# First batch's loads and exponentials placed in the arrays of the later channel weights, with a written list for its steps

## The chip, the cores and the metric

The kernel runs on one NeuronCore of a Trainium2 chip. The metric is the device time of one execution in microseconds, median of three runs. The engines are named as the profile names them: PE is TensorE (matrix products), PEld its weight loads, DVE VectorE, ACT ScalarE, POOL GpSimd, SP SyncE, which only issues DMAs here.

## What is computed

Windowed attention with block summaries, then a mixer over tokens and channels, on four batches of 768 tokens, 8 heads of 64. Cut to what matters:

```
k_sum = max of k over blocks of 32 tokens ; v_sum = mean of v over the same blocks      (24 of each)
a     = softmax over [ q k^T / 8 within |i - j| < 16 ,  q k_sum^T / 8 + log 32 ]
x     = a [v ; v_sum]                     per head; the heads side by side: 768 x 512 per batch
u     = x + (relu(x^T w_tok1) w_tok2)^T   w_tok1 768 x 256, w_tok2 256 x 768
out   = u + relu(u w_ch1) w_ch2           w_ch1 512 x 1536, w_ch2 1536 x 512
```

The weights arrive as 64-bit floats (two 32-bit words each) and are turned into 32-bit ones in the kernel, the channel and second token weights as a high and a low part, so that three fast products stand for one exact one.

## The kernel before

**A plan sets every order.** The code adds pieces of work (`Plan.add`): an engine, an estimated time, what it reads and writes, a rank. `Plan._order` walks them as a small model of the engines would, and the order that comes out is fixed for each engine, SP's queue included. So the places of the instructions follow from the estimates, the ranks and the order in which the pieces are added. A wait at the head of an engine's list holds up all that stands behind it.

**Attention of one pair of heads** (`p`; batch 0 has pairs 0 to 3): `load_k`, `load_q`, `load_v` (L270) bring k (120 columns for each of 12 tiles of 64 queries: a window of 96 keys and 24 places for block maxima), q and two v. `key_blocks` on DVE takes the block maxima (`ks`, L313) and copies them into k (L322). `scores` does one half `g` of the tokens: 12 products into two banks (`sc`, L428), then six times DVE's masked row minimum (L442, called "lowest" here) and ACT's exponential (L452). `turn` transposes the exponentials on PE (`et`, L490), and ACT copies them out (`eT`, L501). `first_means` (batch 0 alone) forms the block means of v on PE (`vm`, 24 products, L340); ACT copies the 24 sums out (`vs`, L360), POOL spreads them into v (L347). `weighted` multiplies with v (`av`, L559) and DVE scales by the reciprocal of the row sums (`x`, L570). An f32 product in the listing is two matrix instructions in the trace: 24 listed are x48 there.

**Token mixer**: `tok1` (`t1p`, L692, ACT L673, DVE L678) and `tok2` (`up`: transposes L849 and products L857; ACT `u` L894, DVE `u` L899).

**Channel mixer**: for each of 12 blocks `f` of the hidden width `ch1` (`hp`, L917, 12 products; ACT and DVE split `h`, L929 and L934) and `ch2` (`acc`, L960, 12 products).

**Weights** come in 30 ticks (`w_tick`): two DMAs (L1092), ACT takes the magnitude (L1122), POOL clamps (L1126), DVE does shift, sign and low word (L1131, L1138, L1145), ACT writes the high part (L1169) and POOL the low one (L1175). Ticks 0 to 5 are token weights, 6 + 2f and 7 + 2f the channel weights of block f. Each tick's words wait in borrowed buffers: tags `u0`, `k`, `q`, `v`, `x`, two buffers each but for `u0` (four).

**The start.** The first steps are added in a loop over a fixed order of scores, turns and products, with the ticks put in at five places; 21 products of a zero tile (`warm`, L1188) run ahead of the first scores. k, q and v have two buffers each, so that the loads for pairs 2 and 3 wait until earlier pairs have been used. The channel weights have four arrays of their own for the whole kernel, `w1h`, `w1l`, `w2h`, `w2l`, which are empty until the ticks fill them. Attention of a later batch is added between the channel steps of the batch ahead of it.

Of the kernel before, what the change touches and what calls it, by code (L numbers as in the profile page):

```python
# [20 lines left out]
DM = H * D  # L21
# [38 lines left out]

class Work:
# [6 lines left out]
class Plan:  # L68
    LATE = {"pe": 0.3, "act": 0.15, "dve": 0.15, "pool": 0.2, "sp": 0.0}
    RATE, LAND = 250.0, 2.2  # L70
# [11 lines left out]
    def add(self, eng, took, run, reads=(), writes=(), rank=0, behind=(), kb=0):  # L82
# [12 lines left out]
        for key in (*reads, *writes):  # L95
            s = key[0]
# [92 lines left out]
def tile_attention_mixer(  # L189
# [77 lines left out]

    def load(slot, view, src, kb, reads=(), behind=()):
# [5 lines left out]
    def load_q(p):  # L274
        b, hp = divmod(p, NP)
        q_t[p] = sbuf([P, S], "q", f"q_{p}", 2)
        return load(q_t[p], lambda t: t, q[b, hp], 393)

    def load_k(p):
        b, hp = divmod(p, NP)  # L280
        k_t[p] = sbuf([P, NT, NC], "k", f"k_{p}", 2)
        return load(k_t[p], lambda t: t, kw[b, hp], 737)

    def load_v(n):
# [5 lines left out]
        tag = "h" if b == 0 and hp % 2 == 1 else "v"  # L290
        slot = v_t[n] = sbuf([P, NT, D], tag, f"v_{n}", 2)
# [37 lines left out]
    def first_means(p):  # L329
# [5 lines left out]
        at = (WIN - 32, WIN)  # L335

        def sums():
            for t in range(NT):
                for j in range(2):
                    nc.tensor.matmul(  # L340
                        pt.t[at[j] : at[j] + NB, :D],
                        lhsT=means[:, NB - 2 - 2 * t : 2 * NB - 2 - 2 * t],
                        rhs=v_t[2 * p + j].t[:WIN, t], start=(t == 0), stop=(t == NT - 1),
                    )

        def spread(n, j):
            nc.gpsimd.tensor_copy(  # L347
                v_t[n].t[WIN:NC],
# [4 lines left out]
            "pe", 1.6, sums, reads=[(v_t[2 * p], 0), (v_t[2 * p + 1], 0)], writes=[(pt, 0)],  # L353
            rank=R_H,
        )
        for j in range(2):
            n = 2 * p + j
            add(
                "act", 0.25,
                lambda j=j: nc.scalar.activation(  # L360
                    s.t[WIN:NC, j * D : (j + 1) * D], pt.t[at[j] : at[j] + NB, :D], AF.Copy
                ),
                reads=[(pt, 0)], writes=[(s, j)], rank=R_EVAC,
            )
# [986 lines left out]
```

## Time and profile before

| what | before |
|---|---|
| median of three runs | 574.99 us (574.8, 574.99, 577.88) |
| profiled execution: span from first to last instruction | 572.0 us |
| around the span (median less span) | 3.0 us |
| PE busy in the span | 561.5 us, 98% |
| DVE, ACT, POOL busy | 278.3, 215.4, 157.9 us |
| mean granted TensorE clock | 0.997 |
| DMA | 75.89 MB, mean 133 GB/s |
| first channel product starts | at 65.31 us |

The profiled execution is one run; its span is what the views below divide up, and the 3.0 us around it are what the runs' times hold besides. Times in views are counted from the span's start. In the chain and the timeline a row reads: start, duration, engine, tile, line, number of instructions. In the tables by stretch, "busy (x)" stands for each engine's busy time and its instructions, then the granted clock, the busy share of the DMA engines and what they moved.

### The profile page before, as it was taken

The page shows a single profiled execution, that of the slowest core. Times are in us where ns is not written, and L with a number is a line of the kernel's source. Part 1 is how long each engine was busy: PE and PEld are TensorE (multiplying, and loading weights), DVE is VectorE, ACT ScalarE, POOL GpSimd, SP SyncE. Part 2 cuts the span into 40 slices and gives each one's busy share as a digit, 9 for nine tenths or more (in the row PEclk, how much of TensorE's full clock was granted, in tenths as well). Part 3 has the DMA queues.
Part 4 walks back from the last instruction along what each step waited for, and adds up shares of the span by engine and source line. Part 5 has one row for each costly group of instructions (what it writes and reads, how often), then busy time and mean ns, then how long its engine had stood idle before and what let it go on. Part 6 is the DMA issues. An engine that isn't in the chain of part 4 may idle for free.

```text
span 572.0 us, 12221 instructions
## 1 busy us (share of the span) xinstructions
PE 561.5 (98%) x4629; PEld 495.9 (87%) x4629; DVE 278.3 (49%) x845; ACT 215.4 (38%) x711; POOL 157.9 (28%) x232
## 2 busy tenths in 40 slices
PE   7899999999999999999999999999999999999997
PEld 3688888889999978877899887878899999999997
DVE  3588899978563364454621455442640422112112
ACT  3776776526474342332314343322423312111110
POOL 0437687824034410000236011100066022005000
PEclk9899999999999999999999999999999999999999
DMA  8953677745465146757856138745542022001001
GB/s 275 325 175 115 204 226 249 251 119 185 152 182 166 37 150 152 208 129 194 220 153 135 16 68 219 198 131 114 136 136 63 14 52 43 1 0 57 0 1 55
DMA packets 116778, 75.89 MB, mean 133 GB/s; under 512 B 86640, under 2 KB 100080, under 8 KB 116720
## 3 DMA queue, kind: packets, MB, share of 16 engines
q1 hardware_dynamic: 116432, 74.72, 46.4%
q8 instruction: 36, 0.59, 0.4%
q10 hardware_dynamic: 288, 0.39, 0.2%
q14 instruction: 22, 0.18, 0.1%
HBM read 57.59 MB, written 15.73 MB: 128 GB/s over the span
## 4 chain that ended last, share of the span: by engine, by line
PE 87%; DVE 3%; ACT 2%; SPq 2%; DMA 2%; POOL 1%; issue 1%; DVEq 0%; ACTq 0%; POOLq 0%
PE hp L917 33%; PE acc L960 33%; PE up L857 5%; PE sc L428 4%; PE av L559 4%; PE t1q L776 3%; SPq L532 2%; PE t1q L739 2%; PE warm L1188 1%; PE et L490 1%; ACT e L452 1%; PE up L849 1%; DMA xT<-xaway 1%; POOL ot L1021 1%; DVE e L442 1%
## 5 line engine op out<-in xcount | busy, mean ns | idle before, releaser
L960 PE MATMUL acc<-h,w2h 128*128 128x512 f32 (+2 forms) x768 | 206.0, 338 | 0.1
L917 PE MATMUL hp<-u,w1h 128*128 128x512 f32 (+2 forms) x768 | 192.8, 338 | 0.0
L960 PEld LDWEIGHTS acc<-h,w2h 128*128 128x128 f32 x768 | 135.5, 188 | 14.0 <-ACT h L929 1.6
L917 PEld LDWEIGHTS hp<-u,w1h 128*128 128x128 f32 x768 | 132.6, 189 | 12.5 <-issue 1.3
L934 DVE SCALAR_TENSOR_TENSOR h<-hp,h 128x512 fp32r<-128x512 f32 (+2 forms) x96 | 53.2, 554 | 156.9 <-ACT h L929 156.7
L917 PE MATMUL hp<-u,w1l 128*128 128x512 f32 (+2 forms) x384 | 129.0, 336 | 0.0
L960 PE MATMUL acc<-h,w2l 128*128 128x512 f32 (+2 forms) x384 | 128.4, 334 | 0.0
L929 ACT ACTIVATE h<-hp 128x512 fp32r<-128x512 f32 (+2 forms) x96 | 47.0, 489 | 199.7 <-PE hp L917 198.7
L452 ACT ACTIVATE e<-e,den 128x120 f32<-128x120 f32 x192 | 73.3, 384 | 55.1 <-DVE den L442 51.8
L917 PEld LDWEIGHTS hp<-u,w1l 128*128 128x128 f32 x384 | 72.4, 189 | 5.8
L960 PEld LDWEIGHTS acc<-h,w2l 128*128 128x128 f32 x384 | 72.2, 188 | 5.3
L442 DVE CUSTOM_DVE_ANT_0 e<-sc,mask_sb 128x120 f32<-128x120 f32 x192 | 41.6, 277 | 20.9 <-PE sc L428 19.7
L1021 POOL TENSOR_TENSOR ot<-ot,u 128x512 f32<-128x512 f32 (+2 forms) x28 | 27.9, 1018 | 84.9 <-DVE ot L1013 83.3
L857 PE MATMUL up<-wt2h,t 128*128 128x256 f32 (+2 forms) x128 | 37.3, 350 | 0.2 <-DVE xT L873 0.2
L452 ACT ACTIVATION_READ_ACCUMULATOR e<-e,den 128x1 f32 x192 | 36.2, 188 | 0.0
L565 POOL TENSOR_SCALAR rec<-den 128x6 f32<-128x6 f32 x32 | 8.6, 269 | 90.8 <-ACT e L452 88.6
L428 PE MATMUL sc<-k,q 64*64 64x120 f32 x768 | 28.1, 273 | 2.2 <-ACT eT L501 0.9
L428 PEld LDWEIGHTS sc<-k,q 64*64 64x64 f32 x768 | 20.5, 133 | 10.5 <-issue 6.1
L559 PEld LDWEIGHTS av<-v,eT 120*64 120x64 f32 x768 | 24.0, 138 | 4.9 <-issue 2.5
L559 PE MATMUL av<-v,eT 120*64 120x64 f32 x768 | 26.6, 224 | 1.0 <-ACT eT L501 0.9
L411 POOL MEMSET e<- 128x48 f32 x16 | 2.2, 139 | 91.4 <-PE av L559 42.0
L857 PEld LDWEIGHTS up<-wt2h,t 128*128 128x128 f32 x128 | 23.1, 188 | 2.6 <-DVE xT L873 0.5
(81 smaller groups left out, 603.4 us busy)
## 6 DMA issues: line engine op xcount, KB each, us to landing
w<-in_w_ch SPq DMA_DIRECT2D x48, 256.0 KB
k<-in_kw SPq DMA_DIRECT2D x16, 720.0 KB
v<-in_vw SPq DMA_DIRECT2D x32, 288.0 KB
q<-in_q SPq DMA_DIRECT2D x16, 384.0 KB
away<-e SPq DMA_DIRECT2D x16, 384.0 KB
eT<-away SPq DMA_DIRECT2D x64, 96.0 KB
w<-in_w_tok SPq DMA_DIRECT2D x12, 256.0 KB
vb<-in_vb SPq DMA_DIRECT2D x32, 96.0 KB
```

The costliest lines, as they stand in the source:

```text
L428: nc.tensor.matmul(tiles[j].t[c * QT : (c + 1) * QT, i * NC : (i + 1) * NC], lhsT=qt.t[rows, t * QT : (t + 1) * QT], rhs=kt.t[rows, t, :], ...
L442: nc.vector.tensor_tensor_reduce(out=e.t[:, j, i * P : i * P + NC], in0=tiles[j].t[:, i * NC : (i + 1) * NC], in1=mask_sb[:, mv, :], op0=A ...
L452: nc.scalar.activation(ei, ei, AF.Exp, bias=den_t[n].t[:, 1, T : T + 1], scale=-1.0, accum_out=den_t[n].t[:, 0, T : T + 1],)
L532: nc.sync.dma_start(out=view()[rows].rearrange("p (t q c) -> p t q c", q=P // 32, c=32), in_=src[..., rows],)
L559: nc.tensor.matmul(pv[cs, T], lhsT=eT[:NC, T % (TT // 2), cs], rhs=v.t[:NC, 2 * T + c], start=True, stop=True,)
L776: nc.tensor.matmul(pt.t.rearrange("p (a c) -> p a c", c=P), lhsT=ws.t[:, wp, T % 2, k * P : (k + 1) * P], rhs=xs.t[:, xp], start=(T == 0 a ...
L857: nc.tensor.matmul(pt.t[:, :nt], lhsT=t1.t[:, part, ks], rhs=w[:, k, h0 : h0 + nt], start=(far and k == 0 and i == 0), stop=(k == DTOK // ...
L917: nc.tensor.matmul(pt.t[:, :nt], lhsT=w[:, c, fs], rhs=us[c].t[:, part], start=(i == 0), stop=(i == len(ops) - 1),)
L929: lambda: nc.scalar.activation(h.t[:, 0], pt.t[:, :nt], AF.Relu),
L934: lambda: nc.vector.scalar_tensor_tensor(out=h.t[:, 1], in0=pt.t[:, :nt], scalar=0.0, in1=h.t[:, 0].bitcast(F32), op0=ALU.max, op1=ALU.sub ...
L960: nc.tensor.matmul(slot.t[:, c0 : c0 + nt], lhsT=w[:, f, o * P : (o + 1) * P], rhs=h.t[:, part], start=(f == 0 and w is w2h and part == 0 ...
L1021: lambda view=view, u=u: nc.gpsimd.tensor_tensor(out=view(), in0=view(), in1=u.t[:, 1].bitcast(F32), op=ALU.add),
```

## The change

Four things are done at once; nothing of what is computed changes.

1. The four channel-weight arrays become 16 tiles of three blocks each. For groups 1 to 3 of each, the same memory first holds a tile of batch 0 (`early`): all four q in group 1 of `w1h` and `w1l`, the four k in group 2 of all four, the eight v in group 3, and in group 1 of `w2h` and `w2l` four of the exponentials (five of the eight steps use these). The weights of a group wait, as the plan sees it, until batch 0's users of that memory are done. With a home of their own, k, q and v of batch 0 need no buffer to come free. The transposed exponentials of batch 0 take the buffers of tags `q` and `v`.
2. The loop of the start becomes a written list of words: `l` loads of a pair, `k` block maxima, `m` block means, `s` scores, `e` turn, `a` weighted, `t` and `u` the token mixer, `w` a tick. Nine ticks stand in it, ten in the loop before. The plan's estimates of the DMA rate (250 to 320), of some steps and of the warm-up change with it.
3. The block means go to four column groups of PE where they went to two: even and odd tiles add up apart. ACT copies the even half out as before, and DVE adds the odd half to it (eight new small additions).
4. 14 warm-up products, 21 before.

```
+    early = {
+        (n, g): plan.slot(sb, [P, WG * DM], F32, f"{n}_{g}", f"early_{n}_{g}", 1)
+        for n in NW for g in range(1, NF // WG)
+    }
...
     def load_k(p):
         b, hp = divmod(p, NP)
-        k_t[p] = sbuf([P, NT, NC], "k", f"k_{p}", 2)
+        if b == 0:
+            k_t[p] = early_part(NW[p], 2, 0, (NT, NC))
+        else:
+            k_t[p] = sbuf([P, NT, NC], "k", f"k_{p}", 2)
...
                 for j in range(2):
+                    c = 2 * j + t % 2
                     nc.tensor.matmul(
-                        pt.t[at[j] : at[j] + NB, :D],
+                        pt.t[32 * c : 32 * c + NB, :D],
                         lhsT=means[:, NB - 2 - 2 * t : 2 * NB - 2 - 2 * t],
-                        rhs=v_t[2 * p + j].t[:WIN, t], start=(t == 0), stop=(t == NT - 1),
+                        rhs=v_t[2 * p + j].t[:WIN, t], start=(t < 2), stop=(t >= NT - 2),
                     )
...
+        def whole(j):
+            nc.vector.tensor_tensor(
+                out=s.t[WIN:NC, j * D : (j + 1) * D], in0=half(j, 1),
+                in1=s.t[WIN:NC, j * D : (j + 1) * D], op=ALU.add,
+            )
...
-        for _ in range(21):
+        for _ in range(14):
             nc.tensor.matmul(pw.t, lhsT=warm.t[:, :P], rhs=warm.t, start=True, stop=True)
...
+    START = (
+        "l0 l1 l2 w k0 k1 s00 s01 s10 e00 k2 s11 w m0 m1 e01 l3 s20 w a0 e10 e11 s21 w e21 "
+        "a1 m2 k3 t1 m3 w w e20 s30 s31 a2 w w t2 e31 e30 t0 u0 u2 a3 u1 t3 w u3"
     )
```

What the plan makes of it is shown at three places. First the head of SP's queue, where all loads are issued; k, q and v carry the pair's or head's number in the old names, and in the new ones the array and group whose memory they take (`early_w1h_2` is k of pair 0, `early_w1l_2` k of pair 1, `early_w2h_2` k of pair 2, `early_w1h_1` q of pairs 0 and 1, `early_w1h_3` v of heads 0 and 1). Before:

```order
L270 DMA k_0_85<-in_kw 128x1440
L270 DMA q_0_87<-in_q 128x768
L1194 DMA mask_sb_71<-in_mask 128x360
L270 DMA k_1_90<-in_kw 128x1440
L270 DMA q_1_92<-in_q 128x768
L270 DMA v_0_94<-in_vw 96x768
L270 DMA v_1_96<-in_vw 96x768
L270 DMA v_2_98<-in_vw 96x768
L270 DMA v_3_122<-in_vw 96x768
L270 DMA k_2_165<-in_kw 128x1440
L270 DMA q_2_167<-in_q 128x768
L1092 DMA w_0_170<-in_w_tok1 128x512 x2
```

The same place now:

```order
L300 DMA early_w1h_2_81<-in_kw 128x1440
L300 DMA early_w1h_1_83<-in_q 128x768
L1253 DMA mask_sb_71<-in_mask 128x360
L300 DMA early_w1h_3_86<-in_vw 96x768 x2
L300 DMA early_w1l_2_89<-in_kw 128x1440
L300 DMA early_w1h_1_83<-in_q 128x768
L300 DMA early_w1l_3_92<-in_vw 96x768 x2
L300 DMA early_w2h_2_110<-in_kw 128x1440
L300 DMA early_w1l_1_112<-in_q 128x768
L300 DMA early_w2h_3_114<-in_vw 96x768 x2
L1147 DMA w_0_117<-in_w_tok1 128x512 x2
L1147 DMA w_1_120<-in_w_tok1 128x512 x2
```

The first nine loads are the same nine; v of heads 0 and 1 has moved ahead of k and q of pair 1, and v of heads 4 and 5 ahead of the token weights.

Second, PE's list around the block means `vm` of pairs 0 and 1 (heads 0 to 3; the exponentials of pair 0 are `e_0` in the old names, `early_w2h_1` in the new). Before:

```order
L340 MATMUL vm_0_230<-v_0_94,means_72 24x64
L340 MATMUL vm_0_230<-v_1_96,means_72 24x64
L490 MATMUL et_0_1_269<-identf_66,e_0_1_177 120x128 x3
L490 MATMUL et_1_1_275<-identf_66,e_0_1_177 120x128 x3
L340 MATMUL vm_1_283<-v_2_98,means_72 24x64
...
L559 MATMUL av_0_313<-v_0_94,eT_0_0_202 64x64 x6
L559 MATMUL av_0_313<-v_0_94,eT_0_1_281 64x64 x6
L559 MATMUL av_1_330<-v_1_96,eT_1_0_205 64x64 x6
L559 MATMUL av_1_330<-v_1_96,eT_1_1_308 64x64 x6
L428 MATMUL sc_2_1_347<-k_1_90,q_1_92 64x120
```

The same place now:

```order
L377 MATMUL vm_1_263<-early_w1l_3_92,means_72 24x64 x24
L540 MATMUL et_0_1_297<-identf_66,early_w2h_1_172 120x128 x3
L482 MATMUL sc_2_1_305<-early_w1l_2_89,early_w1h_1_83 64x120
...
L540 MATMUL et_1_1_327<-identf_66,early_w2h_1_172 120x128 x3
L609 MATMUL av_0_334<-early_w1h_3_86,eT_0_0_238 64x64 x6
L609 MATMUL av_0_334<-early_w1h_3_86,eT_0_1_323 64x64 x6
L609 MATMUL av_1_353<-early_w1h_3_86,eT_0_0_238 64x64 x6
L609 MATMUL av_1_353<-early_w1h_3_86,eT_0_1_323 64x64 x6
L377 MATMUL vm_2_376<-early_w2h_3_114,means_72 24x64 x24
```

The means of pair 1 stand ahead of the second turn of pair 0, and the second half of pair 1's scores, which followed the products with v, stands ahead of them.

Third, SP's queue at the ticks of the third channel block (`w_10`, tick 10) and of the fifth (`w_14`). Before:

```order
L1092 DMA w_12_890<-in_w_ch1 128x2x256 x2
L1092 DMA w_13_933<-in_w_ch2 128x512 x2
L1092 DMA w_10_985<-in_w_ch1 128x2x256 x2
L1092 DMA w_14_0_989<-in_w_ch1 128x2x256
L1092 DMA w_14_1_991<-in_w_ch1 128x2x256
```

The same place now:

```order
L1147 DMA w_12_871<-in_w_ch1 128x2x256 x2
L1147 DMA w_13_898<-in_w_ch2 128x512 x2
L1147 DMA w_14_0_957<-in_w_ch1 128x2x256
L1147 DMA w_14_1_959<-in_w_ch1 128x2x256
L1147 DMA w_10_974<-in_w_ch1 128x2x256 x2
```

Tick 14's two loads, which wait for the words of tick 8 to be used, now stand ahead of tick 10's. On PE, everything from the first `up` on to the end of batch 0's first half stands in nearly the order of before (two `up` have changed places); after that, steps of later batches move by one or two places.

More of the change, by code (lines that the diff above doesn't have):

```diff
@@ L266, in tile_attention_mixer, with early_part, weight, block @@
     q_t, k_t, v_t, vs, vb_t = {}, {}, {}, {}, {}
+    NW, WG = ("w1h", "w1l", "w2h", "w2l"), 3
+    early = {
+        (n, g): plan.slot(sb, [P, WG * DM], F32, f"{n}_{g}", f"early_{n}_{g}", 1)
+        for n in NW for g in range(1, NF // WG)
+    }
+    wt = {
+        (n, g): plan.slot(sb, [P, WG, DM], F32R, f"{n}_{g}", f"{n}_{g}", 1)
+        for n in NW for g in range(NF // WG)
+    }
+    def early_part(n, g, i, shape):
+        size = shape[0] * shape[1]
+        return Part(
+            early[n, g],
+            lambda t: t[:, i * size : (i + 1) * size].rearrange("p (a b) -> p a b", b=shape[1]),
+        )
+    def weight(n, f):
+        return wt[n, f // WG].t[:, f % WG]
+    def block(n, f, c):
+        return weight(n, f)[:, c * P : (c + 1) * P]
     def load(slot, view, src, kb, reads=(), behind=()):
@@ L475, in turn @@
         e = e_t[p, g]
-        if p >= NP:
-            pair = sbuf([P, 2, HS], "e", f"eT_{p}_{g}", 3)
+        tag, bufs = ("e", 3) if p >= NP else (("q", 2), ("v", 2))[g]
+        pair = sbuf([P, 2, HS], tag, f"eT_{p}_{g}", bufs)
         for j in range(2):
@@ L613, in att_step @@
                 turn_x(b, hp)
-            ahead = 1 if b > 0 else 2
-            if b > 0 or hp + ahead < NP:
+            ahead = 1
+            if b > 0:
                 load_v(2 * (p + ahead))
@@ L905, in tile_attention_mixer, with weight_keys @@
     h_t = {}
+    def weight_keys(names, f):
+        return [(wt[n, f // WG], (f, i)) for n in names for i in range(2)]
     def ch1(b, half, f):
@@ L914, in products @@
         def products():
-            ops = [(c, w, part) for c in range(NC4) for w, part in ((w1h, 0), (w1h, 1), (w1l, 0))]
+            ops = [(c, w, part) for c in range(NC4) for w, part in (("w1h", 0), ("w1h", 1), ("w1l", 0))]
             for i, (c, w, part) in enumerate(ops):
                 nc.tensor.matmul(
-                    pt.t[:, :nt], lhsT=w[:, c, fs], rhs=us[c].t[:, part],
+                    pt.t[:, :nt], lhsT=block(w, f, c), rhs=us[c].t[:, part],
                     start=(i == 0), stop=(i == len(ops) - 1),
@@ L923, in ch1 @@
             "pe", 12 * nt / 2220, products,
-            reads=[(u, i) for u in us for i in range(2)] + [("w1", f, 0), ("w1", f, 1)],
+            reads=[(u, i) for u in us for i in range(2)] + weight_keys(("w1h", "w1l"), f),
             writes=[(pt, 0)], rank=R_W,
@@ L1046, in tile_attention_mixer, with halves @@
     w_ch1v = w_ch1.rearrange("(c p) f -> p c f", p=P)
+    def halves(names, f, i):
+        return [lambda n=n: weight(n, f)[:, 256 * i : 256 * (i + 1)] for n in names] + [
+            (wt[n, f // WG], (f, i)) for n in names
+        ]
     for T in range(TT):
-        jobs.append((w_tok1v[:, T : T + 1, :], wt1[:, T - T % 2 : T - T % 2 + 2, :], None, ("wt1", T // 2)))
+        jobs.append((w_tok1v[:, T : T + 1, :], None, None, None, ("wt1", T // 2)))
     for i in range(3):
@@ L1096, in w_tick @@
             )
-        first, rank = two[0][2] is None, R_ATT if i < TOKT else R_W
+        first, rank = two[0][1] is None, R_ATT if i < TOKT else R_W
         psum = i >= 10
```

183 lines of the change are left out of this document (97 added, 86 removed).

## The prediction

> **What bounds the kernel now.** I read the page first, then PE's waits by stretch, then the chain of waits through the first 75 us, then DVE's waits there.
>
> ```profile
> PE 561.5 (98%) x4629; PEld 495.9 (87%) x4629; DVE 278.3 (49%) x845; ACT 215.4 (38%) x711; POOL 157.9 (28%) x232
> PE   7899999999999999999999999999999999999997
> ```
>
> PE is busy nearly throughout; the two slices of 14.3 us that are not full are the first two. PE's longest wait of the start (to 65.3 us), and the only one of all the rest: what waited and for what, total, times, longest:
>
> ```profile
> PE et L490 <- ACT e L452: 2.0, 4, 0.7
> ```
> ```profile
> PE up L857 <- DVE xT L873: 0.2, 1, 0.2
> ```
>
> After 65.3 us PE waits 0.2 us in all: there the time is PE's work, 572.0 - 65.3 = 506.7 us, and the change leaves that work alone. What can be won lies ahead of the first channel product. The chain of waits through the start:
>
> ```profile
> 1.17 7.54 PE warm L1188 x21
> 8.71 0.85 PE sc L428 x24
> 13.16 1.42 PE sc L428 x24
> 14.59 2.69 PE vm L340 x48
> 17.28 0.80 PE et L490 x6
> 18.08 1.46 PE vm L340 x48
> 19.54 1.55 PE av L559 x48
> 21.09 0.78 PE sc L428 x24
> 51.19 0.59 PE up L849 x4
> 56.88 2.68 PE t1p L692 x24
> 65.31 5.46 PE hp L917 x24
> ```
>
> Three marks: scores from 8.7, the first `up` at 51.2, the first channel product `hp` at 65.3. From `up` on the chain is PE alone (14.1 us, the same instructions before and after), so the question is when `up` begins. Between scores and `up` the engines were busy (us, in the first columns):
>
> ```profile
> 9.54:51.80 42.26, 37.09 (x677) 31.55 (x670) 31.83 (x139) 33.53 (x136) 18.99 (x28) 0.96 0.74 229
> ```
>
> 42.3 us, of which PE worked 37.1, DVE 31.8, ACT 33.5. No engine is full; each waits for the others in turn. I take DVE's list as the measure, because it ends with `x` of the last head (51.8), which stands beside the first `up`, and because it is the list to which the change adds work. Its waits in this stretch are 42.26 - 31.83 = 10.4 us:
>
> ```profile
> DVE e L442 <- PE sc L428: 5.8, 3, 3.3
> DVE x L570 <- PE av L559: 4.9, 2, 4.3
> DVE t L678 <- ACT t L673: 1.4, 2, 1.2
> ```
>
> (3.3 of the first row lie ahead of 9.54.) Two of them come early, the second behind slow PE work:
>
> ```profile
> 14.61 0.28 DVE L442 CUSTOM_DVE_ANT_0 e<-sc,mask_sb 128x120 f32<-128x120 f32 x1 [1.35 <-PE sc L428]
> 20.43 0.56 DVE L570 TENSOR_TENSOR x<-av,rec 128x384 f32<-128x384 f32 x1 [4.35 <-PE av L559]
> ```
>
> So 5.7 us are waited up to 20.4 and 4.7 after it.
>
> **The change, part by part.**
>
> *Warm-up.* The 21 products by stretch:
>
> ```profile
> 1.17:7.03 5.86, 5.86 (x14) 2.09 (x15) 1.00 0.89 311
> 7.03:8.64 1.61, 1.61 (x8) 0.59 (x6) 1.00 0.97 380
> ```
>
> The first 14 take 5.86 us (0.42 each), the last seven 1.6 (0.22). Scores wait for nothing else here: k of pair 0 is ready with DVE's copy at 6.25.
>
> ```profile
> 5.94 0.31 DVE L322 COPY k<-ks 128x288 f32<-128x288 f32 x1
> ```
>
> Seven fewer: scores at 7.05 instead of 8.64, **-1.6 us**, all on the path. Bounds: no gain if the mask or q came late (q was issued second, and both queues' places are unchanged), and never more than 1.6.
>
> *Block means.* The row 18.08 has 48 matrix instructions in 1.46 us at full clock, 30 ns each, in two column groups; with four side by side the least is half, 0.73, the most 1.46. The scores use four quarters of the array already: 24 of 120 columns in 0.78 (row 21.09), 33 ns each, which for 64 columns makes 17 ns and 0.84 for 48. I take 0.8. PE saves 0.7 per pair, 2.6 in four, but only pair 1's means stand ahead of a turn that others wait for. The Trainium skill, "TensorE: Matmul & The Clock Gate", section "Wait — 56ns, not 53.3ns?", says that starts of matrix instructions never come closer than about 25 ns, however small they are. By that rule the 48 would take 1.2 us, and as an estimate the total would come out 0.4 us later. The trace shows no four column groups, so the sum keeps 0.8.
>
> *The added half.* ACT's eight small copies stay; DVE gets eight additions of 24x64. None is in the trace; nearest are ACT's copy of the same 24x64 (216 ns) and DVE's reciprocals (178 ns).
>
> ```profile
> L360 ACT ACTIVATE vs<-vm 24x64 f32<-24x64 f32 x8 | 1.7, 216 | 2.9 <-PE vm L340 2.8
> L585 DVE RECIPROCAL rec<-rec 128x6 f32<-128x6 f32 x8 | 1.3, 178 | 0.4 <-POOL rec L565 0.2
> ```
>
> I take 0.2: **+1.6 us** of DVE's list (bounds 1.0 and 2.5).
>
> *Loads at once.* What landed when is bounded by what the DMA engines moved:
>
> ```profile
> 0.00:14.50 14.50, 11.60 (x99) 5.64 (x99) 5.61 (x31) 5.92 (x24) 0.75 (x7) 0.97 0.90 277
> k<-in_kw SPq DMA_DIRECT2D x16, 720.0 KB
> v<-in_vw SPq DMA_DIRECT2D x32, 288.0 KB
> q<-in_q SPq DMA_DIRECT2D x16, 384.0 KB
> mask_sb<-in_mask SPq DMA_DIRECT2D x1, 180.0 KB
> 4.95 0.95 DVE L313 TENSOR_REDUCE ks<-k 128x24 f32<-128x768 f32 x1 [3.19 <-DMA k<-in_kw]
> ```
>
> The engines are 90% busy and move 277 GB/s. The first nine loads (2 k, 2 q, 4 v, mask) are 3540 KB, 3.63 MB, 13.1 us at that rate; the first k (0.74 MB, issued at 0.72) would take 2.7 and was there at 4.95, 1.5 later. So I add 1.5: k of pair 1 is sixth instead of fourth and lands at about 11, its q at 12.4, the last v of pair 1 at 14.6. Loading all at once therefore doesn't speed up the first 15 us; it takes away the later waits of loads for buffers.
>
> Three stretches of 3.4 us, with the granted clock third from the end:
>
> ```profile
> 10.36:13.77 3.41, 1.93 (x21) 1.28 (x25) 2.87 (x20) 3.41 (x17) 0.00 (x0) 1.00 1.07 261
> 13.77:17.19 3.42, 3.42 (x66) 2.94 (x58) 1.47 (x14) 3.00 (x16) 0.47 (x2) 0.50 0.99 357
> 17.19:20.60 3.41, 3.41 (x94) 3.12 (x94) 0.17 (x1) 2.48 (x10) 2.33 (x3) 1.00 0.98 358
> ```
>
> From 13.8 to 17.2 PE has half clock (the mean of 2.69 us against 1.46 and the scores of 1.42 against 0.78 in the chain are from there).
>
> *The new list, early part.* With those landings: DVE starts its minima at 8.0, has done twelve at 10.4 (0.2 each) and the two additions at 10.8, forms pair 1's maxima at 11.1 to 12.3, PE its scores by 13.3, DVE six minima by 14.5: waits 0.3 and 1.0. PE then stands at pair 1's means until 14.6, with pair 0's second turn, pair 1's second scores and the products with v queued behind them. At half clock (below) the means end at 16.0, ACT's copy lets DVE add at 16.5: wait 1.6. Maxima of pair 2 to 18.1, minima and `x` of pair 0 interleaved to 21: wait 0.7. Sum 3.6 us instead of 5.7: **-2.0** (bounds -4.0 with loads 1.5 us early, +1.0 if they land 3 us late).
>
> *The list, later part.* DVE waited 4.7 us between 20.4 and 51.8: for scores behind turns, for `t1p`, for `av`. Now k, q and v of pairs 2 and 3 are there in time: up to tick 3 it is 9.2 MB, of which 3.6 come by 13.1 and the rest at the 357 GB/s above by 29, while ACT's list has at least 22 us of work ahead of that tick and starts at 8.3. And the token products stand later, when their inputs are ready. ACT and DVE are then both nearly full, 33.5 and 33.4 us of a stretch of some 40. I take 2.7 us of waits, between 0.5 and 4.7: **-2.0**.
>
> *Sum.* 8.0 + (31.8 + 1.6) + 3.6 + 2.7 = 47.7 against 51.8: the first `up` comes 4.0 us earlier, `hp` at 61.3. Term by term -1.6 + 1.6 - 2.0 - 2.0 = -4.0.
>
> *After hp.* PE keeps the gain only if the channel weights come as much earlier. The tightest now is the third block: its low words are ready at 72.0, its product starts at 73.5, 1.5 us of slack.
>
> ```profile
> 70.54 1.45 POOL L1175 TENSOR_TENSOR w1l<-wb,w1h 128x256 fp32r<-128x256 f32 x2 [0.31 <-ACT w1h L1169]
> 73.49 2.72 PE hp L917 x12
> ```
>
> DVE, ACT and POOL have the same steps between `up` and there as before, so they move along with `up`. Tick 10's loads go behind tick 14's on SP, which wait for tick 8's words; with `up` as now these are done at 62.9, while tick 10 was issued at 60.7.
>
> ```profile
> 60.73 2.58 SPq L1092 DMA_DIRECT2D w<-in_w_ch  x4
> 61.71 1.16 DVE L1145 SCALAR_TENSOR_TENSOR wb<-w,wb 128x256 int32<-128x256 int32 x2
> 65.63 0.67 ACT L1122 ACTIVATE wb<-w 128x512 f32<-128x512 f32 x1
> ```
>
> That is 2.1 us later, and 3.4 with tick 14's two issues (four took 2.58). At 277 GB/s and with the 1.5 us from above the words of tick 10 then come 3.4 us after their issue, at 67.5 by the old times, 1.9 after ACT used them (65.6). Of that the slack hides 1.5; the 0.4 left is within the error of such a sum, so it goes to the range and not into the sum. Taking the weight arrays in tiles costs nothing: same blocks, same products. Memory shared with the loads is free long before group 1 is needed (fourth block).
>
> The profiled execution's own time is 572.0 + 3.0 = 575.0, the median. **Forecast 575.0 - 4.0 = 571.0 us.** A measurement of this kernel can tell about 0.5% from no change, 2.9 us: faster means under 572.1.
>
> **Rivals.**
>
> *A. The engines pack better* (0.17). Later waits 0.5, loads 1.5 us earlier: another 2.2 + 1.2 us; 567.6. For it: PE has only some 32 us of work in the stretch (37.1 less 2.6, and less 1.9 for half clock). Against: three full lists that wait on each other.
>
> *B. Half clock for a second stretch* (0.20). In the three stretches shown above PE worked 1.9 us of 3.4, then had half clock, worked all of 3.42 and got the clock back. Now PE waits for loads in the same stretch; if that keeps the clock down to 20.6, 1.7 us of work take 3.4, and the later saving shrinks by 0.5: 575.0 - 4.0 + 2.2 = 573.2. The Trainium skill, again "TensorE: Matmul & The Clock Gate", section "What's actually happening", says that the clock rises after a busy window of about 3.4 us and falls after an idle one. By that rule B is the outcome if the window isn't full; the rows above agree with it, with 0.50 and 3.42 of 3.42.
>
> *C. Slower: the third block's weights* (0.06). The second half of tick 8's words now waits for a buffer that transposed exponentials of pair 3 hold until the last products with v. If DVE's waits only change places (10.4 as before), `up` starts at 8.0 + 33.4 + 10.4 = 51.8, as now, and tick 10, behind tick 14, behind tick 8, is 1.9 us late at ACT and one more for each that tick 8 slips. With a slip of 2 us PE waits 1.9 + 2.0 - 1.5 = 2.4 at the third `hp`, all the rest behind it: 577.4. It decides once tick 10's low words come 1.5 us later against `hp` than now; for it speaks the shortest slack of the trace, against it that every step between has the same work.
>
> That the loads don't come earlier at all is no rival: it is the forecast for the first nine.
>
> **How the numbers follow.** The forecast has 0.57 (own range 569.0 to 573.0; 0.43 of it under 572.1). A 0.17 faster, B 0.20 (0.02 faster, 0.18 same), C 0.06 (0.02 same, 0.04 slower). Faster 0.62, same 0.34, slower 0.04. The range 567.0 to 574.8 holds the forecast's whole case, most of A and B, and leaves out C and the ends of both.
>
> **What would show it.** Right: scores at about 7.1; pair 1's means at 14 to 15 after a wait of PE; 48 instructions of a mean in about 0.75 us; first `up` near 47.5, `hp` near 61.3, no wait after it. Wrong: PE waits between `hp` and `acc` for POOL's low words (C); half clock up to 20.6 (B); DVE waits after 21 us of 4 us or more, or below 1 (A); k of pair 1 before 10 us, which breaks the landing sum.

## The result and the profile after

| | before | after |
|---|---|---|
| median, same chip, four runs each | 576.38 us (574.8 to 577.88) | 589.04 us (588.76 to 590.52) |
| ratio, 95% interval | | 1.0237 (1.0203 to 1.027): slower |
| profiled execution: span, around it | 572.0, 3.0 us | 587.1, 1.8 us |
| first `up`, first channel product `hp` (chain) | 51.19, 65.31 us | 53.94, 67.89 us |
| mean granted clock | 0.997 | 0.988 |

The forecast was 571.0. Where a run beside the experiments has its span on record, its time is 1.7 to 2.1 us more than the span; by that (an estimate) before's profiled run took about 574 us, some 2.5 less than the median here, so that the spans differ by more (15.1) than the medians (12.7). How long PE has only half its clock also differs between runs of one kernel: of 110 runs of before beside the experiments, 61 have a mean granted clock of 0.996 or 0.997 and a median of 574.2 us, 38 have 0.987 to 0.991 and 576.6. A profile is one run, and before's is of the first kind. In after's listing the lines have moved: means `vm` L377, scores L482, turns L540, `av` L609, `up` L899 and L907, `hp` L970, `acc` L1013. The page of after, busy time by engine and PE in 40 slices:

```profile
PE 563.6 (96%) x4622; PEld 495.4 (84%) x4622; DVE 278.9 (48%) x853; ACT 216.6 (37%) x711; POOL 156.2 (27%) x232
PE   7779999999999998999989998999999999999997
```

Three weak slices at the head instead of two, and in the middle three slices that are no longer full, where before had none. The main ones of PE's waits in after's whole span (what waited and for what; total, times, longest):

```profile
PE av L609 <- DMA eT<-away: 5.5, 3, 2.1
PE vm L377 <- DMA early_w2l<-in_vw: 3.7, 2, 2.9
PE vm L377 <- DMA early_w2h<-in_vw: 2.0, 2, 1.2
PE et L540 <- DVE den L496: 1.2, 1, 1.2
PE et L540 <- ACT e L506: 1.1, 2, 0.7
PE vm L377 <- DMA early_w1h<-in_vw: 1.1, 2, 0.8
PE av L609 <- PE hp L970: 0.7, 1, 0.7
```

Two families: the block means of batch 0 wait for v (`vm`, 6.8 us, all at the start), and the products with v of later batches wait for exponentials that come back over DMA (`eT<-away`, 5.5 us, all after `hp`). Before's profile has neither. The whole loss divides at `hp`. From `hp` to the end (length; PE, PEld, DVE, ACT, POOL busy; clock; DMA share; GB/s), after:

```profile
67.89:587.10 519.21, 507.06 (x3816) 448.94 (x3815) 230.81 (x679) 172.01 (x554) 129.23 (x186) 1.00 0.43 119
```

and before:

```profile
65.31:572.00 506.69, 502.59 (x3816) 448.81 (x3815) 232.85 (x681) 172.24 (x554) 129.51 (x187) 1.00 0.44 121
```

So the span's +15.1 us are **+2.6 ahead of `hp` and +12.5 behind it**. Of the 12.5, PE's time without work grew from 4.1 to 12.1 (**8.0**; the waits for `eT` are 5.5 of it, five other waits 2.5), and the same 3816 matrix instructions took 507.1 instead of 502.6 (**4.5**). The stretch that the prediction held to be untouched has five sixths of the loss.

**The start of after.** The chain of waits, its rows for the means, the first `up` and the first `hp`:

```profile
9.14 13.56 DMA early_w2h<-in_vw
22.72 9.93 DMA early_w2l<-in_vw
32.70 1.49 PE vm L377 x46
53.94 0.59 PE up L899 x4
67.89 5.59 PE hp L970 x24
```

The chain now runs through loads: v of pair 2 until 22.7, v of pair 3 until 32.7, then PE. The same columns as above, for the stretch of the loads and that behind it, and for the two stretches at half clock with the one between them:

```profile
6.31:32.70 26.39, 16.41 (x363) 12.44 (x363) 18.43 (x95) 19.73 (x86) 7.62 (x12) 0.86 1.04 299
32.70:53.94 21.24, 21.24 (x335) 19.61 (x336) 14.47 (x50) 15.61 (x53) 10.87 (x17) 0.85 0.35 116
11.84:18.67 6.83, 5.93 (x102) 4.52 (x102) 3.07 (x19) 5.25 (x23) 2.75 (x5) 0.51 1.04 291
18.67:32.33 13.66, 6.81 (x160) 5.23 (x158) 11.27 (x51) 10.78 (x45) 3.95 (x6) 0.99 1.04 292
32.33:39.15 6.82, 6.46 (x103) 5.57 (x103) 2.77 (x9) 3.35 (x12) 2.81 (x6) 0.51 0.89 295
```

Up to 32.7 the DMA engines are full at 299 GB/s and PE works 16.4 of 26.4 us; then PE has no idle time at all until `up`. Half clock fills 13.6 us, where before's profile had 3.4.

SP's queue shows why pair 3 is last (its rows between 10 and 23 us, and its longest wait for a load there):

```profile
10.83 3.99 SPq L1147 DMA_DIRECT2D w<-in_w_tok  x4
18.33 0.33 SPq L300 DMA_DIRECT2D early_w2l<-in_kw  x1
21.53 1.52 SPq L300 DMA_DIRECT2D early_w2l<-in_vw  x2
SPq L300 <- DMA early_w2h<-in_kw: 3.5, 1, 3.5
```

The words of two ticks go ahead of pair 3's loads. And k of pair 3 (`early_w2l`), whose memory is free from the start, is issued only when k of pair 2 (`early_w2h`) has landed, the eighth load before it on the queue. All of SP's waits for a landing up to there are of this kind, for the eighth load before.

**Behind `hp`.** One of the three waits, on PE's timeline (start, length, instruction, wait ahead of it) of after:

```profile
228.37 0.57 PE L609 MATMUL av<-v,eT 120*64 120x64 f32 x12
230.80 1.27 PE L609 MATMUL av<-v,eT 120*64 120x64 f32 x36 [1.86 <-DMA eT<-away]
```

and SP's queue of after ahead of it, the exponentials' store and the loads that bring them back:

```profile
219.08 0.33 SPq L567 DMA_DIRECT2D away<-e  x1
221.49 2.77 SPq L582 DMA_DIRECT2D eT<-away  x4
225.03 2.67 SPq L582 DMA_DIRECT2D eT<-away  x4
```

The last of the eight loads is issued by 227.7; the product that needs them stands 0.7 us later, and gets them at 230.8. The plan put it there: it now reckons with 320 instead of 250 KB per us for every load, not only those of the start.

### The profile page after: what moved, and what is told of

Same layout as the page of the kernel before. It is cut to its first block, busy times and chain, and to the rows that moved or that the text cites. A ratio compares the mean times of both kernels' runs of the same rounds, so it can differ in the third digit from the quotient of the medians.

```text
span 587.1 us, 12198 instructions
## 1 busy us (share of the span) xinstructions
PE 563.6 (96%) x4622; PEld 495.4 (84%) x4622; DVE 278.9 (48%) x853; ACT 216.6 (37%) x711; POOL 156.2 (27%) x232
## 4 chain that ended last, share of the span: by engine, by line
PE 79%; DMA 11%; SPq 5%; DVE 2%; ACT 1%; issue 1%; POOL 1%; DVEq 0%; ACTq 0%
PE acc L1013 30%; PE hp L970 29%; PE up L907 5%; PE av L609 4%; SPq L582 4%; PE t1q L826 3%; PE sc L482 3%; DMA early_w2h<-in_vw 2%; PE t1p L742 2%; DMA early_w2l<-in_vw 2%; DMA eT<-away 2%; DMA away<-e 2%; PE t1q L789 2%; PE et L540 1%; DMA early_w1h<-in_vw 1%
## 5 line engine op out<-in xcount | busy, mean ns | idle before, releaser
L1013 PE MATMUL acc<-h,w2h 128*128 128x512 f32 (+2 forms) x768 | 207.6, 340 | 0.0
L970 PE MATMUL hp<-u,w1h 128*128 128x512 f32 (+2 forms) x768 | 192.7, 338 | 0.0
L1013 PEld LDWEIGHTS acc<-h,w2h 128*128 128x128 f32 x768 | 135.6, 188 | 14.4 <-ACT h L982 2.2
L970 PEld LDWEIGHTS hp<-u,w1h 128*128 128x128 f32 x768 | 132.6, 188 | 13.0 <-issue 0.8
L970 PE MATMUL hp<-u,w1l 128*128 128x512 f32 (+2 forms) x384 | 129.2, 336 | 0.0
L1013 PE MATMUL acc<-h,w2l 128*128 128x512 f32 (+2 forms) x384 | 129.1, 336 | 0.0
L970 PEld LDWEIGHTS hp<-u,w1l 128*128 128x128 f32 x384 | 72.1, 188 | 6.3
L1013 PEld LDWEIGHTS acc<-h,w2l 128*128 128x128 f32 x384 | 72.2, 188 | 5.3
L506 ACT ACTIVATE e<-e,den 128x120 f32<-128x120 f32 x162 | 61.9, 384 | 32.6 <-DVE den L496 31.6
L907 PE MATMUL up<-wt2h,t 128*128 128x256 f32 (+2 forms) x128 | 37.5, 351 | 0.5 <-DVE den L496 0.3
L496 DVE CUSTOM_DVE_ANT_0 e<-sc,mask_sb 128x120 f32<-128x120 f32 x162 | 35.0, 276 | 2.4 <-PE sc L482 2.2
L430 DVE TENSOR_REDUCE vs<-vb 96x8 f32<-96x256 f32 (+1 forms) x40 | 18.1, 462 | 28.6 <-DMA vb<-in_vb 28.1
L506 ACT ACTIVATION_READ_ACCUMULATOR e<-e,den 128x1 f32 x162 | 30.6, 189 | 0.0
L465 POOL MEMSET e<- 128x48 f32 x16 | 2.2, 139 | 97.7 <-PE av L609 53.9
L609 PEld LDWEIGHTS av<-v,eT 120*64 120x64 f32 x576 | 18.2, 138 | 10.2 <-issue 6.3
L609 PE MATMUL av<-v,eT 120*64 120x64 f32 x576 | 20.3, 224 | 6.6 <-DMA eT<-away 5.5
L907 PEld LDWEIGHTS up<-wt2h,t 128*128 128x128 f32 x128 | 23.1, 188 | 3.4 <-DVE xT L923 0.7
L1177 ACT ACTIVATE wb<-w 128x512 f32<-128x512 f32 (+1 forms) x35 | 19.1, 563 | 14.9 <-DMA w<-in_w_ch 10.8
```

The lines of the kernel that those rows point to most:

```text
L430: lambda: nc.vector.tensor_reduce(out=s.t[:VB, rows], in_=slot.t[:VB], axis=AX, op=ALU.add),
L496: nc.vector.tensor_tensor_reduce(out=e.t[:, j, i * P : i * P + NC], in0=tiles[j].t[:, i * NC : (i + 1) * NC], in1=mask_sb[:, mv, :], op0=A ...
L506: nc.scalar.activation(ei, ei, AF.Exp, bias=den_t[n].t[:, 1, T : T + 1], scale=-1.0, accum_out=den_t[n].t[:, 0, T : T + 1],)
L609: nc.tensor.matmul(pv[cs, T], lhsT=eT[:NC, T % (TT // 2), cs], rhs=v.t[:NC, 2 * T + c], start=True, stop=True,)
L907: nc.tensor.matmul(pt.t[:, :nt], lhsT=t1.t[:, part, ks], rhs=w[:, k, h0 : h0 + nt], start=(far and k == 0 and i == 0), stop=(k == DTOK // ...
L970: nc.tensor.matmul(pt.t[:, :nt], lhsT=block(w, f, c), rhs=us[c].t[:, part], start=(i == 0), stop=(i == len(ops) - 1),)
```

## The experiments

Seventeen kernels, each beside runs of before on the same chip; ratios are against those. "Late" is the work that the plan adds behind the written list.

**e1: the late rate undone.**

```diff
+    plan.RATE = 250.0        # behind the loop over START
     start = [sum(HT[0][j // NF] // 256 for j in range(i)) for i in range(2 * NF + 1)]
```

(each piece of work keeps the rate that held when it was added)

> The kernel after, with the plan's DMA rate at 250 again for all work added behind the start list; the start itself is reckoned at 320 as in the change, so everything up to the first channel product keeps its order. Theory R (the reckoned rate of 320 puts later products ahead of their transfers): PE's waits after hp fall from 8.0 us to under 2, the first hp stays at 67 to 68.5, and the time is 9 to 11 us under the kernel after, 578 to 580. Rival M (the new homes of the weights, or contention, cost the 12 us): waits or longer products stay, 587 to 589.

578.7 us (577.2 to 580.0), ratio 1.0067 (1.0044 to 1.009): 10.3 us less than after's median. PE's waits of e1 behind 66 us, all of them:

```profile
PE av L611 <- PE hp L972: 0.7, 1, 0.7
PE acc L1015 <- ACT h L984: 0.7, 1, 0.7
PE up L909 <- DVE xT L925: 0.2, 1, 0.2
```

The waits for `eT` are gone. The same pair on e1's timeline of PE:

```profile
228.88 1.62 PE L611 MATMUL av<-v,eT 120*64 120x64 f32 x48
```

and in e1's queue of SP:

```profile
219.21 2.77 SPq L584 DMA_DIRECT2D eT<-away  x4
222.72 2.66 SPq L584 DMA_DIRECT2D eT<-away  x4
```

The loads end at 225.4 and the products stand 3.5 us behind them instead of 0.7. From `hp` to the end e1 has

```profile
66.72:577.70 510.98, 505.60 (x3818) 448.96 (x3816) 232.85 (x680) 172.30 (x554) 129.38 (x186) 1.00 0.44 120
```

that is 5.4 us without work on PE (after 12.1) and 1.5 us less work. Theory R holds; `hp`, at 66.7, came a little earlier than it said.

**e2: the same edit the other way.** Before, with 320 behind the start.

```diff
+    plan.RATE = 320.0        # before.py, which has 250 throughout
     start = [sum(HT[0][j // NF] // 256 for j in range(i)) for i in range(2 * NF + 1)]
```

> The kernel before, with the plan's DMA rate at 320 for all work added behind the start; the start keeps its order and its 250. Theory R: hp at 65.3 as before, then PE waits of 4 to 9 us, most of them products with v for exponentials that come back over DMA; 6 to 10 us slower than before. Rival M: within 1 us of before.

588.17 us (585.0 to 591.6), ratio 1.0225 (1.0182 to 1.0268). PE's first wait in e2 behind 66 us:

```profile
PE av L561 <- DMA eT<-away: 6.7, 3, 2.9
```

The one number turns before into a kernel as slow as after, with the same wait, and costs more than the 6 to 10 us expected (13.5). That the late rate is the cause is shown from both sides.

**e3: 250 everywhere in after.**

```diff
-    RATE, LAND = 320.0, 2.2
+    RATE, LAND = 250.0, 2.2
```

> The kernel after, with the plan's DMA rate at 250 throughout; the list of words, the homes, the means and the 14 warm-ups stay. Theory R for the start as well (block means reckoned too early stand at the head of PE's list and wait for v): PE's waits for v of 6.8 us shrink to under 2, first hp at 62 to 65, total 572 to 577. Rival L (the loads themselves hold up the start, whatever the order): hp still at 66 to 68.5, total 578 to 580.

581.23 us, ratio 1.0117 (1.0076 to 1.0158). PE's waits for v shrink from 6.8 to 0.8, as meant, but at the start others come (DVE `t` 2.0, POOL `wt` 2.0, DVE `u` 1.6), and `hp` starts at 71.25, later than in after (67.7 on the same timeline). The theory that the plan's rate also explains the start falls.

**e4 and e5: the warm-up.** Before with 14, and e1 with 21:

```diff
-        for _ in range(21):      # e4; e5 the reverse, on e1
+        for _ in range(14):
```

> The kernel before with 14 warm-up products and nothing else. By the prediction's term scores start 1.6 us earlier and the time falls by 1.6 at most; if the first loads or the clock give it back, the time is within 0.5 us of before. Its trace also shows whether products of 512 columns start 227 ns apart on this chip too (then the 231 ns seen after are the change's) or are 0.5 to 1% slower by the chip.

> The first experiment's kernel (after, later work reckoned at 250) with 21 warm-up products again and the same order everywhere. Theory K (with 14 warm-ups scores start ahead of the loads, PE's work has holes and the granted clock stays at half for 6.8 us at a time instead of 3.4): the first stretch of half clock falls to about 3.4 us, first hp no later or up to 2 us earlier than the 67.2 of the first experiment, total 576.5 to 578.5. Rival: the clock follows the waits for v and not the warm-up: two stretches of 6.8 us again, hp 1 to 1.6 us later, 579.5 to 580.5.

e4: 575.42 us, ratio 0.9999 (0.9976 to 1.0022). e5: 579.54, ratio 1.0073 (1.0047 to 1.0099), e1's within error; its first half clock is 3.4 us long as theory K said, but the second stays 6.8 and `hp` comes at 67.1, no earlier than in e1. In e4 the scores start at 6.2 instead of 8.7, and `up` at 51.87 instead of 51.19. Its stretches at half clock:

```profile
11.80:18.67 6.87, 6.52 (x97) 5.59 (x94) 1.47 (x14) 4.71 (x22) 2.07 (x4) 0.52 1.03 342
25.50:32.30 6.80, 6.10 (x78) 4.61 (x79) 6.12 (x21) 2.86 (x11) 3.15 (x4) 0.51 0.94 312
```

13.7 us of half clock in this run, where before's profile has 3.4: its earlier scores met the same waits. Not every run of e4 is like that. Four of the twelve have before's clock of 0.997 and take 572.3 to 573.8 us, median 573.2; on this chip the ten runs of before at 0.997 have 574.2. So some of the earlier start is kept where the clock is, and the medians of all runs hide it.

**e6: pair 3's loads ahead of the token weights** (on e1).

```diff
-        "l0 l1 l2 w k0 k1 s00 s01 s10 e00 k2 s11 w m0 m1 e01 l3 s20 w a0 e10 e11 s21 w e21 "
+        "l0 l1 l2 l3 w k0 k1 s00 s01 s10 e00 k2 s11 w m0 m1 e01 s20 w a0 e10 e11 s21 w e21 "
```

> The first experiment's kernel with the loads of pair 3 (k, q and both v, 1.7 MB) ahead of the first two ticks' words instead of behind them. Theory V (PE stands at the block means of pair 3 because its v is still on the way, 3.9 us in the first experiment): v of pair 3 lands at 26 to 28 instead of 32, the wait shrinks to under 1 us, hp comes at 63 to 65.5, total 574.5 to 577. Rival W (the ticks' words, now later, hold up ACT, DVE and the token products instead): hp at 66.5 to 68.5, 578 to 580.

581.89 us, ratio 1.0111 (1.0066 to 1.0155); `up` at 54.4, `hp` at 72.1. Waits for v are 4.4 us (e1: 5.2), and `t1p` then waits 2.1 for DVE: the wait moved, and `up` came 1.6 us later than in e1.

**e7: the tiles alone, on before.**

```diff
-    w1h = const.tile([P, NC4, DFF], F32R, name="w1h")
...
+    wt = {(n, g): const.tile([P, 3, DM], F32R, name=f"{n}_{g}")
+          for n in ("w1h", "w1l", "w2h", "w2l") for g in range(NF // 3)}
```

> The kernel before with its four channel weight arrays taken as 16 tiles of three blocks, nothing shared and no order changed. Theory T (where the tiles lie sets how far apart the channel products start): products of 512 columns start 229 to 233 ns apart for some blocks instead of 227, about 2 us slower than before (0.2 to 0.5%). Rival: the 231 ns come from the shared memory or the moved buffers and not from tiling: 227 ns and within 0.5 us of before.

574.83 us, ratio 0.998 (0.996 to 1.0): no cost. Its products of 512 columns start 227 ns apart by the median, as before's do, so theory T falls.

**e8 and e11: the four-group means alone, on before.** In e8 the additions are pieces of their own for the plan; in e11 they ride with ACT's copy, and the order of before stays.

```diff
-                        pt.t[at[j] : at[j] + NB, :D],
+                        pt.t[32 * c : 32 * c + NB, :D],
...
+            add("dve", 0.2, lambda j=j: whole(j), reads=[(pt, 0)], writes=[(s, j)], rank=R_EVAC)
```

> The kernel before with the block means in four column groups and the eight DVE additions, nothing else (21 warm-ups, old loop, old loads). By the prediction's terms: 48 instructions of a mean in 0.80 us at full clock (by a 25 ns spacing it would be 1.2), an addition 0.2 us, time within 0.8 us of before on either side. Rival: the addition between ACT's copy and POOL's spreading holds up the first products with v, and hp comes 1 to 2 us later.

> The kernel before with four column groups for the block means as in the last experiment, but every piece in the order of before (each DVE addition is put where ACT's copy stands in the plan). Theory O (the 7 us that the last experiment lost between up and hp came from the reshuffled order and not from the means): hp at 64 to 65.3, total 0.3 to 1.5 us under before. Rival: the eight additions hold up DVE and POOL themselves: hp at 66 or later, over 1 us slower than before.

e8: 582.78 us, ratio 1.0108 (1.0071 to 1.0145). The plan's order shifted all through the start; PE's longest wait in e8:

```profile
PE t1p L700 <- DVE u L907: 4.9, 1, 4.9
```

So e8 measures an order, not the means. e11: 575.89, ratio 1.0013 (0.9994 to 1.0033): the means by themselves are worth nothing here, where theory O had 0.3 to 1.5 us under before. Its profiled run has `hp` at 66.6, with 10.2 us of half clock ahead of it.

**e9: less v.** e1 with one of twelve tiles of v of pairs 2 and 3 loaded, the rest set to zero (so that part of the input is left out).

```diff
+                nc.gpsimd.memset(slot.t[:WIN, 1:], 0.0)
+                nc.sync.dma_start(out=slot.t[:WIN, :1], in_=vw[b, h][:, :1])
```

> The first experiment's kernel in the same order on every engine, but of the v of pairs 2 and 3 only one tile in twelve is loaded and the rest is set to zero by POOL at the start, so that this v is there early (it leaves that data out). Theory V (PE stands at the block means for v): the waits of PE for v fall from 5.2 us to under 1, first up at 47.5 to 49.5 instead of 52.8, first hp 62 to 64, total 573.5 to 575.5. Rival K (the waits only change places: scores wait for k and q, exponentials for ACT, and the clock stays at half): first up 51 to 52.5, total 577 to 578.5.

578.21 us, ratio 1.0049 (1.0028 to 1.0071); the waits for v of pairs 2 and 3 are gone (1.1 for pair 0's is left), and `up` starts at 50.8 instead of 52.8, not at the 47.5 to 49.5 of theory V. Half clock still fills 17.0 us.

**e10: unused products in the holes.** e1 with 23 products of the zero tile ahead of the places where PE waits.

```diff
         def sums():
+            fill(pt.t, (2, 0, 5, 12)[p])
...
+            if (p, g) == (1, 0):
+                fill(tiles[0].t, 4)
```

> The first experiment's kernel in the same order, with 23 unused products of the zero tile put where PE waits: 2 ahead of the means of pair 0, 4 ahead of the first scores of pair 1, 5 ahead of the means of pair 2, 12 ahead of those of pair 3. Theory K (PE's holes let the clock fall to half, 13.6 us of it, and that costs 4 us or more): half clock for under 4 us in all, first up at 48 to 50.5, total 574.5 to 576.5. Rival V (the clock hardly matters because PE waits for v anyway): first up at 52 to 54, total 578 to 580.

577.78 us, ratio 1.0055 (1.0033 to 1.0078). Half clock shrinks from 13.6 to 3.4 us, though v of pair 3 is issued at the same time (22.07 against 22.10); `up` at 50.8, again 2.0 earlier. All eight runs have a clock of 0.996 to 1.0, where e1's eight have 0.985 to 0.991, and e15 and e17 below, with the same fillers, start `up` at 51.1 and 50.7. The time gains less than the 2 us: 0.9 by the medians, 0.7 by the ratios, within error and short of theory K.

**e14: both, e9 and e10.**

```diff
+            fill(pt.t, (2, 0, 5, 12)[p])
+                nc.sync.dma_start(out=slot.t[:WIN, :1], in_=vw[b, h][:, :1])
```

> The tenth experiment's kernel (unused products in PE's holes) with the short v of the ninth (the data of pairs 2 and 3 is left out but for one tile in twelve), same order. Each alone brought the first up from 52.8 to 50.8. Theory S (waits for v and half clock are two prices that add): first up at 48.3 to 49.3, hp at 62.5 to 63.5. Rival E (what PE has to do after the token weights arrive sets the end): first up at 50.3 to 51, hp at 64.6 to 65.3.

576.63 us, ratio 1.0033 (1.002 to 1.0047), `up` at 50.0: together 2.7, not 4.0. From 36 us to `up`, e10:

```profile
36.00:50.77 14.77, 14.63 (x232) 13.75 (x221) 12.38 (x44) 11.99 (x43) 9.66 (x14) 1.00 0.22 71
```

and e14:

```profile
36.00:50.01 14.01, 13.88 (x207) 13.15 (x205) 11.65 (x43) 11.62 (x42) 8.92 (x13) 1.00 0.12 40
```

PE is full (13.88 of 14.01) and at full clock. What came earlier ran up against PE's own work at the end of the start.

**e12: filling before's own holes.** Seven unused products in before, ahead of pair 0's first turns and pair 1's scores.

```diff
+                if (p, g) == (0, 0):
+                    fill(pt.t, (3, 2)[j])
...
+            if (p, g) == (1, 0):
+                fill(tiles[0].t, 2)
```

> The kernel before in its own order with seven unused products in PE's holes at 10 to 13 us: 3 and 2 ahead of the first two turns, 2 ahead of the first scores of pair 1. Theory K: no half clock from 13.8 to 17.2 us, which gives PE 1.9 us back there; hp 0.5 to 1.9 us earlier, total 573 to 574.5 against 575. Rival: the half clock only comes later or DVE and ACT set the pace; within 0.5 us of before.

576.64 us, ratio 1.0028 (1.0008 to 1.0048). The profiled run has no half clock in its start and `hp` at 64.8 (0.3 earlier than before on the timeline), but then 2.5 us of waits of `av` for `eT`, which before's profile doesn't have. Of the twelve runs six have a clock of 0.990 to 0.993; the six at 0.999 or 1.0 have a median of 574.9, no better than before's 574.2 at its full clock. So the fillers didn't keep the clock in every run, and where they did nothing was won.

**e13 and e15: places in memory.** The products of 512 columns in after stand 231 to 233 ns apart in some blocks and 227 in others; in before 227 by the median throughout. The addresses in the compiled kernels hint at the operands' places: in before the moving and the stationary operand of all of these products lie at the same place modulo 256 bytes, in after half of them don't (42% differ modulo 128; the 68% of the expectation below doesn't come out). First theory: 128 bytes suffice. e13 is e1, e15 is e10, with every buffer rounded to 128 bytes.

```diff
+        per = 128 // (2 if dtype == F16 else 4)
+        flat = pool.tile([shape[0], -(-n // per) * per], dtype, tag=self.tag, name=name, bufs=self.bufs)
```

> The first experiment's kernel with every buffer rounded up to a multiple of 128 bytes per partition, so that the moving and the stationary operand of every channel product start at the same place modulo 128 (in the kernel after, 68% of those with 512 columns do not; in before all do). Nothing else is changed. Theory A (unequal places make the products of 512 columns start 230 to 233 ns apart instead of 227): 227 ns in all blocks, 1.5 to 2.5 us under the first experiment. Rival: the spacing has another cause; 229 to 233 ns stay, time as in the first experiment, 578 to 579.5.

> All that can be kept of the change with what the experiments point to: the kernel after, later work reckoned at 250, unused products in PE's holes, buffers rounded up to 128 bytes. By the parts: 577.8 of the tenth experiment less about 2 us, 575.5 to 576.5, level with before within 0.3%. Rival: the clock or the exponentials that come over DMA take it back, 577 to 578.

e13: 580.47 us, ratio 1.0099 (1.0082 to 1.0115); e15: 578.84, ratio 1.0073 (1.0058 to 1.0088). No gain; in e13 products whose places differ by 128 modulo 256 start 232 ns apart by the median, those at equal places 227. The 128-byte theory falls.

**e16 and e17: equal places modulo 256 bytes**, on e1 and e10.

```diff
+        per = (128 if self.tag in ("ks", "rec", "den") else 256) // (2 if dtype == F16 else 4)
+        bufs = 6 if self.tag == "den" else self.bufs
```

> The first experiment's kernel with the buffers rounded so that the moving and the stationary operand of every channel product lie at the same place modulo 256 bytes (the round to 128 of the thirteenth experiment left 0 in some blocks and 128 in others, and those with 0 had 227 ns, those with 128 had 231 to 233). Order as before. Theory A2 (equal places modulo 256 bytes decide): 227 ns in all blocks of 512 columns but for the first products behind a change, 1.5 to 2.5 us under the first experiment, 576 to 577.5. Rival: the match was chance; 229 to 233 ns stay and the time is 578 to 580.

> The tenth experiment's kernel (later work reckoned at 250, unused products in PE's holes) with the same rounding modulo 256. By the parts: 577.8 less about 2 us, 575.5 to 576.5, within 0.4% of before. Rival: the products keep 231 ns, 577.5 to 579.

e16: 577.72 us, ratio 1.0056 (1.0038 to 1.0074). Twelve products of 512 columns in the chain (start, length), in before:

```profile
92.53 2.72 PE acc L960 x12
95.25 2.72 PE hp L917 x12
```

in after:

```profile
95.49 2.79 PE acc L1013 x12
98.29 2.77 PE hp L970 x12
```

and in e16:

```profile
95.11 2.72 PE acc L1027 x12
97.83 2.72 PE hp L984 x12
```

2.79 and 2.77 against 2.72 for twelve are 4 to 6 ns each, about 2%. From `hp` to the end of e16:

```profile
66.47:574.70 508.23, 503.44 (x3818) 449.47 (x3816) 232.04 (x680) 172.15 (x554) 128.66 (x186) 1.00 0.44 121
```

PE's work is 2.2 us less than e1's (505.6) in the same instructions, though the time is only 1.0 less by the medians, on another chip, and 0.6 by the ratios. The rule modulo 256 isn't the whole of it: in after itself the products at equal places start 229 ns apart by the median, those at unequal ones 231 to 233. What the rounding does is shown, and why is open. e17: 575.87 us, ratio 1.0013 (0.9991 to 1.0034), level with before; e10, on the same chip and without the rounding, has 577.78. No kernel here is clearly faster than before.

## Why the prediction was wrong

**"After 65.3 us ... the change leaves that work alone": this step failed, and it carries the sign.** The instructions are the same, their order isn't. The text on the change names the rate of 320, as a part of the new start, and says that later steps move "by one or two places"; the prediction gives neither a price. Yet that is enough: the products with v now stand 0.7 us behind the issue of their loads, 3.5 us with the old rate (e1). Price 10.3 us (e1; 9.8 by the ratios, 1.0237 less 1.0067), with the reverse at 588.17 against before's 574.64 (e2). The prediction had looked for waits behind `hp` in one place only, the third block's weights (rival C); those didn't wait.

**"Taking the weight arrays in tiles costs nothing": true of the tiles (e7), false of what they displace.** The buffers move to other addresses, and rounding them to 256 bytes takes 2.2 us off PE's work (e1 against e16).

**"k, q, v of pairs 2 and 3 are there in time": failed.** The first nine loads were forecast right. PE's timeline in after has the means of pairs 0 and 1:

```profile
9.17 0.86 PE L377 MATMUL vm<-early_w1h,means 96*24 96x64 f32 x46 [0.79 <-DMA early_w1h<-in_vw]
14.15 1.85 PE L377 MATMUL vm<-early_w1l,means 96*24 96x64 f32 x48
```

Pair 1's start at 14.15 for a forecast of 14.6, at half clock, and end at 16.0 as reckoned. But the rest was put at 357 GB/s, the rate of one stretch of 3.4 us, and came at 292 (the row from 18.67, 13.7 us): the 5.6 MB that were left behind 13.1 us take 19.2 us at that rate, to 32.3. v of pair 3 landed at 32.7 instead of by 29. The loads no longer wait for a buffer, but for the eighth load before them.

**DVE's list as the measure: failed.** It holds until the last v; from 32.7 PE is busy 21.24 of 21.24 us, and `up` waits for PE. DVE's own waits were mis-sized too: put at 3.6 up to 21 us and 2.7 behind it, they are 4.7 and 9.1 (to 53.9). So the -2.0 for the later waits was no gain but a loss. What the start lost can be priced: waits for v 2.0 us alone (e9), half clock 2.0 alone (e10), 2.7 together (e14). With v short and the holes filled, `up` comes at 50.0, still 2.5 later than the 47.5 forecast.

**Warm-up, -1.6: the scores came even earlier, the gain didn't.** They start at 6.3 for a forecast of 7.05, since the 14 products took 4.99 us and not 5.86. Before with 14 is 575.42 against 574.64 (e4); only its runs at a clock of 0.997 are some 1 us faster than before's.

**Rival B happened, and larger.** It reckoned with 6.8 us of half clock in all; there were 13.6, two stretches of 6.8. Each is two periods of 3.41: in the first of them PE still waits (busy 2.46 us of 3.41 from 11.66 on, 2.85 from 32.14 on), and the clock comes back behind the second, which was worked through (3.42 of 3.42 both times). The Trainium skill, "TensorE: Matmul & The Clock Gate", section "What's actually happening", has the clock rise after a busy window of about 3.4 us; these rows agree. e10, which puts unused products into the waits, agrees in all its runs; e12 does so in half of them.

**Sizes.** 0.8 for a four-group mean was right: 46 instructions in 0.86 us, 19 ns each with the tail of the last. The Trainium skill, same page, section "Wait — 56ns, not 53.3ns?", has starts never closer than about 25 ns; here the measurement decides, and they are closer. The additions, forecast at 0.2:

```profile
L391 DVE TENSOR_TENSOR vs<-vm,vs 24x64 f32<-24x64 f32 x8 | 1.8, 225 | 4.8 <-ACT vs L388 4.7
```

Both sizes were right and worth nothing in the time (e11); in after PE even waits 0.7 us once for an addition.

**The account.** By the ratios, each kernel with one edit more than the last, after's 13.6 us over before shrink by 9.8 with the late rate undone (e1), by 0.7 with the holes filled (e10, within error) and by 2.4 with the buffers rounded (e17); 0.7 are left, within error. Taken in another order the parts differ: the rounding alone, on e1, gives 0.6 (e16). The 2.0 to 2.7 us that e10 and e14 win at `up` are therefore not all found again at the end.

**Open.** Why rounding the buffers to 256 bytes makes the products start closer was not found, only that it does. What else would lower the 50 us at which `up` starts wasn't tried: it would take less PE work between 33 us and `up`. Why e17 stays level with before, with `hp` at 65.0 as before's (65.1), is answered only in part: PE's work behind `hp` there is 504.1 us against 502.6.

## What to carry to other kernels

Where a planner writes the order, its cost numbers are part of the change: ask of each number which work it touches far from the edit, and try that number alone first. Before crediting a load with "in time", take the rate from a long stretch, look what stands ahead of it on the queue, and look who is full once it has landed. An engine that starts earlier only to wait for the same inputs wins little, as the scores did here. And read the granted clock of all runs before a stretch at half clock in one profile is put down to an edit.

## What the hardware showed that was not expected

- f32 products of 512 columns started 227 ns apart where all buffers that PE reads for them lay at equal places modulo 256 bytes (before, e7, e16, e17), and 231 to 233 at unequal places; where both kinds were mixed, in after, those at equal places had 229. Those of 256 columns were the other way round by 2 ns (in before 120 at equal places, 118 at unequal).
- Half clock came in stretches of 3.41, 6.83 or 10.24 us, and how much of it there is differs between runs of the same kernel (before: mean clock 0.987 to 0.997).
- Small products in four column groups started less than 19 ns apart.
- On SP's queue a load was issued only when the eighth load before it had landed, however free its own memory was (after, up to 33 us; k of pair 3 stood 3.5 us for that). Whether the chip or the way the kernel is built sets the eight, no run here shows.
